# The last output tile of a fused attention and feed-forward kernel, computed by column blocks

## The chip, the cores and the metric

The kernel runs on one core of a Trainium2 chip. The metric is device microseconds of one execution; the figure given for a kernel is the median over runs. Engines are TensorE (PE in the profile; its weight loads are PEld), VectorE (DVE), ScalarE (ACT), GpSimd (POOL) and SyncE (SP), which issues the stores.

## What is computed

Attention in a sliding window over 8 batches of 8 heads, 576 positions and 64 dimensions, whose output, as 4608 rows of 512, goes through a two-layer network with a smooth ReLU between the layers:

```python
def _attn_ref(q, k, v):
    scores = scale * np.matmul(q, k.transpose(0, 1, 3, 2))
    mask = np.abs(pos[:, None] - pos[None, :]) <= 32
    attn = softmax(np.where(mask, scores, -1e9))
    return np.matmul(attn, v)

def _moe_ref(x, w_in, w_out):          # x: 4608 x 512, w_in: 512 x 2048, w_out: 2048 x 512
    h = x @ w_in
    g = np.where(h >= 1, h, np.where(h <= -1, 0.0, (h + 1) ** 2 / 4))
    return g @ w_out                   # 4608 x 512, float32
```

## The kernel before

The work is a software pipeline over 152 steps (the loop over `a` at the end of the kernel; 18 token blocks of 256 tokens, 8 steps each, and 8 steps more). In step `a` the first layer's product for block `t = a // 8` and 256 hidden columns `f = a % 8` is formed: eight matmuls of 256 columns into the PSUM tile `hp` (L441). ScalarE (L445) and VectorE (L447, L448) turn it into two of the 16 slices of `gT[t]`, bf16, hidden units on the partitions. Attention of later batches (scores, sums, transposes) is laid into the early and middle steps by a list written by hand (`ev`, `tps`, `xps`); its last events fall at step 128.

The second layer's product runs eight steps behind, in `quarter(x)`. The output has 36 tiles of 128 tokens by 512 columns; tile `tt` takes four calls, `x = 4 * tt` to `4 * tt + 3`. Call `ff` multiplies slices `4 * ff` to `4 * ff + 3` of `gT[tt // 2]` (the weights that are loaded, 128x128) with the rows of `w_out` (512 columns that stream), and adds to the PSUM tile `op`: four matmuls of 512 columns on L412. `op` is 128 x 512 f32, which is one PSUM bank, and the pool `ps_o` has two of them. When all 16 slices are summed, ScalarE copies the tile to SBUF (`osb`, L417, three buffers) and SyncE stores it (L418), 256 KB in 128 rows of 2 KB. SyncE's queue holds nothing else near the end.

In steps 144 to 151 there is no first-layer work any more: the eight calls for tiles 34 and 35 run one after the other. Tile 35 is the last, calls 140 to 143 in steps 148 to 151. After it stand the closing waits and the barrier of the program (L494), where SyncE waits for each DMA semaphore in turn.

All engines take their instructions in program order; the order is the order of the calls, and the waits between engines follow from the tiles that the instructions write and read.

Of the kernel before, what the change touches and what calls it, by code (L numbers as in the profile page):

```python
# [15 lines left out]
def kernel(  # L16
# [19 lines left out]
    nc = tc.nc  # L36
    B, H, S, D = q.shape
    NT, DM, DFF = out.shape[0], 512, 2048
# [31 lines left out]
    w_out = const.tile([128, 16, DM], BF, name="w_out")  # L70
# [4 lines left out]
    V, P, A = nc.vector, nc.gpsimd, nc.scalar  # L75
# [287 lines left out]
    NF = DFF // 256  # L363
# [39 lines left out]
    gT, op = {}, {}  # L403

    def quarter(x):

        tt, ff = divmod(x, 4)
        if tt not in op:
            op[tt] = ps_o.tile([128, DM], FP, name="op", tag="op"), []
        o, done = op[tt]  # L410
        for j in range(4 * ff, 4 * ff + 4):
            nc.tensor.matmul(o, gT[tt // 2][:, j, 128 * (tt % 2):128 * (tt % 2) + 128], w_out[:, j],  # L412
                             start=not done, stop=len(done) == 2 * NF - 1, skip_group_check=True)
            done.append(j)
        if len(done) == 2 * NF:
            osb = osp.tile([128, DM], FP, name="osb")
            A.copy(osb, o)  # L417
            nc.sync.dma_start(out=out[128 * tt:128 * tt + 128, :], in_=osb)  # L418

    for a in range(NF * NB + NF):  # L420
        t, f = divmod(a, NF)
# [27 lines left out]
        for x in pre:  # L449
            quarter(x)  # L450
# [9 lines left out]
        for x in post:  # L460
            quarter(x)
# [37 lines left out]
```

## Time and profile before

| what | us |
|---|---|
| median of 4 runs | 323.26 |
| lowest, highest | 322.52, 324.16 |
| the profiled execution | 323.3 |
| its span (first to last instruction) | 321.5 |
| TensorE busy | 306.4 (95%) |
| VectorE busy | 246.5 (77%) |
| ScalarE busy | 194.5 (60%) |
| 576 matmuls of L412, busy | 146.6 |
| one copy of an output tile (L417) | 0.58 |
| one store of an output tile, issue to landing, median | 2.4 |

The profile is of one execution. [...] The chain of waits follows the work that ended last back from the end. A line in a timeline gives start, length, engine, line, what is written and read, how many, and in brackets how long the engine stood idle before and who ended that.

### The profile page before, as it was taken

To read this page: it belongs to the slowest core of one execution; us is meant where nothing else is said; L and a number is where in the kernel's file an instruction comes from. 1 tells how busy PE (TensorE), PEld (TensorE's weight loads), DVE (VectorE), ACT (ScalarE), POOL (GpSimd) and SP (SyncE) were. 2 spreads that over 40 slices of the span, in tenths; PEclk is the share of its full clock that TensorE was granted. 3 is DMA by queue.
4 is the path that set the end of the run, shared out by engine and by line. 5 is a ranking of instruction groups with operands and counts; after the bars stand their busy time and mean duration, and the time that the engine had idled before them with its cause. 6 is when DMAs were issued, how large, how long until landed. Compare 5 with 4: busy or idle time off the path is not lost.

```text
span 321.5 us, 8537 instructions
## 1 busy us (share of the span) xinstructions
PE 306.4 (95%) x3643; PEld 202.2 (63%) x3643; DVE 246.5 (77%) x384; ACT 194.5 (60%) x320; POOL 86.3 (27%) x120
## 2 busy tenths in 40 slices
PE   8949799999999999999999999999999999999995
PEld 3537655666666666666666666666666666666652
DVE  2335975887888898888888888888888888887760
ACT  3647765676776566766666667566666766554421
POOL 8972937897204603222320300000000000000000
PEclk9998999999999999999999999999999999999999
DMA  9999999999999999929991936005320010000111
GB/s 147 141 155 190 146 176 124 200 151 165 151 162 157 165 125 178 160 55 101 191 162 47 108 87 128 35 33 108 79 65 33 35 35 36 33 35 33 46 54 65
DMA packets 121029, 34.52 MB, mean 107 GB/s; under 512 B 108704, under 2 KB 116128, under 8 KB 120992
## 3 DMA queue, kind: packets, MB, share of 16 engines
q0 software_dynamic: 92128, 18.06, 72.5%
q1 hardware_dynamic: 28864, 15.93, 20.5%
q8 instruction: 28, 0.46, 0.6%
q14 instruction: 9, 0.07, 0.1%
HBM read 36.70 MB, written 9.44 MB: 143 GB/s over the span
## 4 chain that ended last, share of the span: by engine, by line
PE 83%; DVE 5%; DMA 3%; ACT 3%; POOL 3%; issue 1%; POOLq 0%; ACTq 0%
PE op L412 38%; PE hp L441 36%; PE bb L284 6%; DMA w_in<-in_moe_w_in_dram 3%; PE bb L218 2%; DVE mx L447 2%; DVE gT L448 1%; POOL vn L101 1%; PE tp L179 1%; POOL kn L85 1%; DVE xT L296 1%; ACT lr L290 1%; ACT rc L291 1%; ACT pt L226 1%; POOL w_in L105 1%
## 5 line engine op out<-in xcount | busy, mean ns | idle before, releaser
L441 PE MATMUL hp<-xT,w_in 128*128 128x256 bf16 x1152 | 150.2, 274 | 4.1 <-DVE xT L299 1.3
L412 PE MATMUL op<-w_out,gT 128*128 128x512 bf16 x576 | 146.6, 380 | 0.0
L445 ACT ACTIVATE rr<-hp 128x512 f32<-128x512 f32 x144 | 85.5, 595 | 91.8 <-PE hp L441 88.5
L441 PEld LDWEIGHTS <-w_in 128*128 128x128 bf16 x1152 | 111.9, 98 | 46.2 <-issue 4.8
L447 DVE TENSOR_TENSOR mx<-hp,rr 128x512 f32<-128x512 f32 x144 | 99.3, 690 | 42.5 <-ACT rr L445 40.3
L448 DVE SCALAR_TENSOR_TENSOR gT<-rr,mx 128x512 bf16<-128x512 f32 x144 | 99.7, 692 | 4.9
L412 PEld LDWEIGHTS <-gT 128*128 128x128 bf16 x576 | 53.2, 98 | 41.7
L226 ACT ACTIVATE pt<-bb 128x1024 bf16<-128x1024 f32 (+1 forms) x33 | 33.1, 1010 | 6.0 <-PE bb L218 4.8
L101 POOL DMA_DIRECT2D vn<-in_v_dram x32 | 27.6, 882 | 30.3 <-PE bb L218 28.9
L296 DVE TENSOR_TENSOR xT<-bb,rc 128x512 bf16<-128x512 f32 (+1 forms) x32 | 21.1, 658 | 11.3 <-ACT rc L291 10.8
L417 ACT COPY osb<-op 128x512 f32<-128x512 f32 x36 | 20.8, 581 | 11.6 <-PE op L412 11.2
L291 ACT ACTIVATE rc<-lr 128x512 f32<-128x512 f32 (+2 forms) x40 | 23.5, 587 | 1.3
L93 POOL DMA_DIRECT2D qn<-in_q_dram x10 | 12.3, 1240 | 40.8 <-DMA qT<-qn 40.8
L290 ACT ACTIVATE lr<-bb 128x512 f32<-128x512 f32 (+2 forms) x40 | 22.0, 550 | 1.4 <-PE bb L284 1.3
L193 DVE TENSOR_TENSOR pt<-pt,mask 128x1024 bf16<-128x1024 bf16 (+1 forms) x34 | 20.9, 616 | 0.2 <-ACT pt L226 0.2
L284 PE MATMUL bb<-pt,ones 64*64 64x256 bf16 (+3 forms) x352 | 19.5, 256 | 1.5 <-DVE xT L296 0.6
L284 PE MATMUL bb<-pt,vn 64*64 64x128 bf16 (+3 forms) x712 | 18.2, 204 | 0.0
L284 PEld LDWEIGHTS <-ones 64*64 64x64 bf16 x352 | 10.5, 105 | 10.4 <-issue 9.4
L284 PEld LDWEIGHTS <-vn 64*64 64x64 bf16 x712 | 16.7, 107 | 0.0
L85 POOL DMA_DIRECT2D kn<-in_k_dram x24 | 13.0, 554 | 11.0 <-DMA w_in<-in_moe_w_in_dram 3.2
L218 PE MATMUL bb<-qT,kT 64*64 64x128 bf16 x520 | 13.4, 220 | 0.8 <-DVE kT L182 0.8
L93 POOL DMA_DIRECT2D kn<-in_k_dram x10 | 12.1, 1219 | 3.3 <-DMA kn<-in_k_dram 1.9
(44 smaller groups left out, 98.1 us busy)
## 6 DMA issues: line engine op xcount, KB each, us to landing
out_dram<-osb SPq DMA_DIRECT2D x36, 256.0 KB, 2.4
vn<-in_v_dram POOLq DMA_DIRECT2D x32, 144.0 KB, 5.1
qn<-in_q_dram POOLq DMA_DIRECT2D x10, 288.0 KB, 7.5
kn<-in_k_dram POOLq DMA_DIRECT2D x10, 288.0 KB, 8.9
w_out<-in_moe_w_out_dram POOLq DMA_DIRECT2D x4, 512.0 KB, 9.5
kn<-in_k_dram POOLq DMA_DIRECT2D x24, 72.0 KB, 4.8
w_in<-in_moe_w_in_dram POOLq DMA_DIRECT2D x6, 256.0 KB, 7.6
qn<-in_q_dram POOLq DMA_DIRECT2D x20, 72.0 KB, 4.7
```

The costliest lines, as they stand in the source:

```text
L93: nc.gpsimd.dma_start(out=x[:, :, h], in_=src[b, NY * h:NY * h + NY].rearrange("y s d -> (y s) d") .rearrange("(u p) d -> p u d", p=128))
L101: nc.gpsimd.dma_start(out=vn[b][64 * a:64 * a + 64, :, h], in_=v[b, y:y + 2].rearrange("y s d -> (y s) d") .rearrange("(c r) d -> r c d", ...
L226: A.activation(p, ps[:, :, :128 * n].rearrange(like, y=m), AF.Exp, scale=D ** -0.5)
L284: nc.tensor.matmul(bb[HD[h], a, o + c0:o + c1], ones[HD[a]] if c is None else vn[b][HD[a], c, h], p(a, h), start=n == 0, stop=True, skip_g ...
L290: A.activation(lr[:, :, :D0], bb[:, :, D0:2 * D0], AF.Ln)
L291: A.activation(rc[:, :, :D0], lr[:, :, :D0], AF.Exp, scale=-1.0)
L296: muls.append(lambda: V.tensor_mul(o, bb[:, :, :D0], rc[:, :, :D0]))
L412: nc.tensor.matmul(o, gT[tt // 2][:, j, 128 * (tt % 2):128 * (tt % 2) + 128], w_out[:, j], start=not done, stop=len(done) == 2 * NF - 1, s ...
L441: nc.tensor.matmul(hp[:, j], w_in[:, kk, 256 * f + 128 * j:256 * f + 128 * j + 128], xT[:, kk, r0:r0 + TB], start=n == 0, stop=n == 3)
L445: A.activation(rr, hp, AF.Relu, scale=0.5, bias=0.5)
L447: V.tensor_max(mx, hp, rr)
L448: V.scalar_tensor_tensor(gT[t][:, 2 * f:2 * f + 2], rr, 1.0, mx, op0=ALU.min, op1=ALU.mult)
```

## The change

Only the last tile (`tt == 35`) is affected. Each of its four calls now does all 16 slices for 128 of the 512 output columns (block `ff`: columns `128 * ff` to `128 * ff + 127`), as 16 matmuls of 128 columns, in place of 4 slices for all 512 columns. After each call ScalarE copies these 128 columns to a new `osb` buffer and SyncE stores them, 64 KB in 128 rows of 512 bytes. All four blocks are parts of the same PSUM tile `op`. The other 35 tiles are as before.

```diff
-        for j in range(4 * ff, 4 * ff + 4):
-            nc.tensor.matmul(o, gT[tt // 2][:, j, 128 * (tt % 2):128 * (tt % 2) + 128], w_out[:, j],
-                             start=not done, stop=len(done) == 2 * NF - 1, skip_group_check=True)
+        rows, last = slice(128 * tt, 128 * tt + 128), tt == NT // 128 - 1
+        c = slice(128 * ff, 128 * ff + 128) if last else slice(0, DM)
+        for j in range(2 * NF) if last else range(4 * ff, 4 * ff + 4):
+            nc.tensor.matmul(o[:, c], gT[tt // 2][:, j, 128 * (tt % 2):128 * (tt % 2) + 128], w_out[:, j, c],
+                             start=j == 0 if last else not done, stop=j == 2 * NF - 1 if last else len(done) == 2 * NF - 1,
+                             skip_group_check=True)
             done.append(j)
-        if len(done) == 2 * NF:
+        if last or len(done) == 2 * NF:
             osb = osp.tile([128, DM], FP, name="osb")
-            A.copy(osb, o)
-            nc.sync.dma_start(out=out[128 * tt:128 * tt + 128, :], in_=osb)
+            A.copy(osb[:, c], o[:, c])
+            nc.sync.dma_start(out=out[rows, c], in_=osb[:, c])
```

In instructions: 16 matmuls of 512 columns become 64 of 128, each with its weight load; one copy of 512 columns becomes four of 128; one store becomes four.

## The prediction

> **What bounds the kernel now.** I read the page's chain of waits by line first (TensorE holds 83% of the span), then the same chain over the last 16 us, because the edit touches one output tile of 36, the last.
>
> ```profile
> 308.95 0.87 PE hp L441 x8
> 309.82 7.78 PE op L412 x36
> 317.61 0.02 issue
> 317.63 0.58 ACT osb L417
> ```
>
> The columns are start, length, what. From 309.82 on nothing is on the chain but the output product: four matmuls of an earlier quarter, then 32 of tiles 34 and 35. After these stands one copy, and then nothing that computes. So every nanosecond that the last tile gains or loses is a nanosecond of the span; there is no other work to hide it. The timeline after the last matmul starts shows the rest of the path:
>
> ```profile
> 317.21 0.38 PE L412 MATMUL op<-w_out,gT 128*128 128x512 bf16 x1
> 317.63 0.58 ACT L417 COPY osb<-op 128x512 f32<-128x512 f32 x1 [2.87 <-PE op L412]
> 318.24 0.33 SPq L418 DMA_DIRECT2D out_dram<-osb  x1
> ```
>
> The last matmul ends at 317.59, ScalarE starts 0.04 later, its copy takes 0.585, the store is issued 0.03 after it and lands 2.00 after its issue (the answer on the tile osb has 2.0). SyncE waits for it until 320.26, goes through the rest of its list of closing waits until 320.69, and the closing barrier ends at 321.5. The profiled execution took 323.3 us, 1.8 beyond its span, and stands 0.04 above the median of the four runs (323.26, from 322.52 to 324.16).
>
> The first matmul of tile 35 starts 15 pitches before the last one. The pitch follows from the 36 matmuls that run from 309.66 to 317.59: (7.93 - 0.38) / 35 = 0.216 us. So tile 35 now takes, from its first matmul to the end of its copy, 15 x 0.216 + 0.379 + 0.037 + 0.585 = 4.24 us.
>
> **The matmuls.** 16 of 512 columns become 64 of 128, so the 128x128 blocks of gT are loaded 64 times and not 16. What does a load with a matmul of 128 columns cost in a stream? One row has just this shape:
>
> ```profile
> 6.58 0.67 PE L181 MATMUL tp<-ident,qb 128*128 128x128 bf16 x9
> L181 PEld LDWEIGHTS <-qb x9: 96/98/98, 6.4 to 7.0; 128*128 128x128 bf16 x9
> L181 PE MATMUL tp<-ident,qb x9: 219/219/220, 6.6 to 7.0; 128*128 128x128 bf16 x9
> ```
>
> Nine of them take 0.67 us, and the last alone 0.22: (0.67 - 0.22) / 8 = 0.056 each, with a full load in front of every one. A load is shown as 98 ns, but loads and matmuls overlap: the pitch is a quarter of 0.216 and 2 ns more. Those nine are transposes; the upper bound for matmuls into f32 sums is a load that doesn't overlap the next, 0.098. I take 0.056. Then 63 x 0.056 + 0.220 = 3.75 stands against 15 x 0.216 + 0.379 = 3.62.
>
> [...]
>
> **The copy.** ScalarE reads 128 columns at a time. The narrowest rows of f32 from PSUM:
>
> ```profile
> L290 ACT ACTIVATE lr<-bb 128x512 f32<-128x512 f32 x16 | 9.5, 593 | 0.0
> L290 ACT ACTIVATE lr<-bb 128x384 f32<-128x384 f32 x8 | 3.9, 485 | 0.6 <-PE bb L284 0.6
> L249 ACT ACTIVATE pt<-s 128x192 bf16<-128x192 f32 x2 | 0.5, 332 | 0.0
> ```
>
> (593 - 485) / 128 = 0.84 ns for a column, so 384 columns fewer save 0.32 and a copy of 128 takes 0.585 - 0.324 = 0.26. Bounds: 0.146 (a quarter, no fixed part) and 0.332 (the row of 192). Without any wait added, tile 35 would take 3.75 + 0.037 + 0.26 = 4.05: **0.19 less than now**.
>
> **The wait that the change adds.** All four column blocks lie in one PSUM tile, one bank. Block 1 starts to be written when block 0 has to be read. In the old kernel nowhere is a PSUM tile read while TensorE still has to write into it: each reader takes a finished tile, and the next one goes to another buffer. So the trace can't show the case. The nearest row is TensorE refilling a bank that another engine is reading:
>
> ```profile
> 37.37 0.68 DVE L447 TENSOR_TENSOR mx<-hp,rr 128x512 f32<-128x512 f32 x1
> 38.11 0.27 PE L441 MATMUL hp<-xT,w_in 128*128 128x256 bf16 x1 [0.72 <-DVE mx L447]
> ```
>
> The matmul stood 0.72 us until the reader was done, and began 0.05 after its end. There the columns were the same; here they differ. Ends for the change: no wait, or the first matmul of each of blocks 1 to 3 waits for the copy of the block before. I take the wait, because the bank is the unit in that row. Queued behind the waiting matmul are the 15 others of its block, and behind these the next copy and store: all on the path. Each hand-over then costs the end of the last matmul (0.220), ScalarE's start (0.037), the copy (0.26) and TensorE's restart (0.053), less the pitch that would have been there (0.056): 0.51. **Three of them: +1.54.** With the -0.19 this makes +1.35 to the end of the last copy. The cover by the next block's matmuls that column blocks might have is thus gone; only the stores of blocks 0 to 2 lie beside later work.
>
> [...]
>
> TensorE's idle share also bears on its clock. It would stand still for about a quarter of tile 35 (1.5 of 5.6 us). In the stretch 16 to 20 us it was busy 1.88 of 4 us and the granted clock stayed 1.00, so I cost this at nothing; a halved clock over the last two blocks would add 32 x 0.056 = 1.8.
>
> **The store.** The last one carries 128 rows of 512 bytes and not of 2 KB. In the stretch 319 to 320 the old one shows:
>
> ```profile
> DMA packets 144, 0.26 MB, mean 262 GB/s; under 512 B 16, under 2 KB 16, under 8 KB 144
> q1 hardware_dynamic: 144, 0.26, 70.0%
> ```
>
> That is 0.70 us of 16 DMA engines, 8 data packets on each, 0.087 a packet. The page's row of that queue over the whole span (28864 packets, 15.93 MB, 20.5% of 16 x 321.5 us) has, after 4608 such packets are taken off, 24256 smaller ones of 268 bytes and 27 ns in the mean. On a line between the two, 512 bytes take 35 ns: 8 x 0.035 = 0.28, so the landing comes **0.42 earlier**. Bounds: nothing (a packet costs the same), -0.52 (a quarter of the time). Three more issues of 0.33 on SyncE's queue lie 1.4 us apart and wait for nobody. Each block takes a new osb of three: block 2 needs that of tile 34, whose store was issued at 314.79 and landed at 316.80, a microsecond ahead; block 3 needs that of block 0, also landed by then. No wait there.
>
> **The closing waits.** The stores take eight semaphores in turn, and SyncE's closing list asks for them in that order, 0.061 each in the trace. Now the last store has the second of the eight, and six more are asked for after it landed. Three more stores make it the fifth, with three behind it: **-0.18** (bounds 0 and -0.18).
>
> **Sum:** +1.35 - 0.42 - 0.18 = +0.75. On the profiled execution 323.3 + 0.75 = 324.05, a span of 322.25; on the median 324.0.
>
> **The rivals.**
> 1. No wait by bank. For it: the columns are disjoint. Against it: the refill row. Then -0.19 - 0.42 - 0.18 = -0.79: 322.5.
> 2. The weight loads become the bound. Place: inside each block. Price: with 0.098 a pair, 60 pitches x 0.042 = +2.5, in all +3.3: 326.5, slower. It decides from a pitch of about 0.070 on, where 60 x 0.014 lifts the sum over half a per cent. For it: the load's 98 ns; against it: the nine at 0.056.
> 3. The split does less than it says at the end: the small store lands no earlier and the list of waits is as long. Then +1.35: 324.6.
>
> **How the numbers follow.** A measurement of this kernel tells about 0.5%, 1.6 us, from no change; the four runs shown differ by that much. Chances: my forecast 0.68, at 323.3 to 324.6 by the bounds on copy and store; rival 3 0.14; rival 1 0.08; rival 2, from 0.070 on, 0.10. The range 322.8 to 325.2 holds the first two with the scatter of the runs and leaves out nearly all of the other two. Slower by over 0.5%: rival 2 and a corner where copy and store are both at their upper bounds, 0.11. Faster by over 0.5%: no case reaches it, 0.02. Within: 0.87.
>
> **What would show it.** In the new profile: three idle times of about 0.5 us before L412 matmuls, put down to the copy; a period of 1.41 us from block to block; a pitch of 0.056 inside; copies of 0.26; a last copy ending at about 319.56; its store landing about 1.6 after its issue. I am wrong if those idle times are missing, if the pitch is near 0.1, or if a copy starts before its block is done.

## The result, and the profile after

The changed kernel takes 324.42 us (median of 44 runs) beside 323.51 (63 runs of the old kernel): the ratio is 1.0032, 95% interval 1.0021 to 1.0042. That is 0.7 to 1.4 us more, where +0.75 was forecast; the measured time lies within the range, and within half a per cent of the old one.

The profiled executions differ by only 0.2 us (323.52 beside 323.3; spans 321.7 and 321.5), because the new one was 0.63 us ahead at its 48th matmul of the first layer, at about 30 us, and 0.62 at the last one. The edit doesn't touch that part of the program; in the traces below, which begin with the same code but for the last three, that 48th matmul starts anywhere from 29.65 to 31.63. So every trace below is measured from the start of the last matmul of the first layer, which the edits don't touch: 12.82 us to the end of the span now, 11.99 before. The first stage of the table takes 4.43 in every trace of this document.

| stage, us | old | changed | difference |
|---|---|---|---|
| last first-layer matmul to first matmul of tile 35 | 4.43 | 4.43 | 0.00 |
| from there to the end of the last copy | 4.24 | 5.71 | +1.47 |
| from there to the landing of the last store | 2.03 | 1.59 | -0.44 |
| from there to the end of the span | 1.30 | 1.10 | -0.20 |
| sum | 11.99 | 12.82 | **+0.83** |

The chain of the changed kernel over its last microseconds (start, length, what):

```profile
309.20 5.22 PE op L414 x36
314.42 0.02 issue
314.44 0.27 ACT osb L420
314.72 0.04 issue
314.76 1.07 PE op L414 x16
315.83 0.03 ACTq L420
315.86 0.04 issue
315.90 0.27 ACT osb L420
316.17 0.04 issue
316.21 1.07 PE op L414 x16
...
318.80 0.27 ACT osb L420
```

Where the old chain had one unbroken TensorE piece up to the single copy, matmuls and copies now alternate: 16 matmuls, a copy, 16 matmuls, with a period of 1.45 us. The waits of the same stretch say who holds whom (in total, times, longest), and below them stands TensorE's timeline:

```profile
ACT osb L420 <- PE op L414: 6.7, 5, 2.9
...
PE op L414 <- ACT osb L420: 1.1, 3, 0.4
```

```profile
314.76 1.05 PE L414 MATMUL op<-w_out,gT 128*128 128x128 bf16 x16 [0.35 <-ACT osb L420]
316.21 1.05 PE L414 MATMUL op<-w_out,gT 128*128 128x128 bf16 x16 [0.40 <-ACT osb L420]
317.66 1.05 PE L414 MATMUL op<-w_out,gT 128*128 128x128 bf16 x16 [0.40 <-ACT osb L420]
```

The wait of PE for ACT is new. TensorE, which waited for nothing in the old kernel's end, stands idle three times (0.35, 0.40, 0.40). The 16 matmuls of a block take 1.05: 15 pitches of 0.056 and 0.22 for the last one. The idle time is less than the cost of a hand-over (0.55), because the profile counts the end of the last matmul as busy (0.22 shown for it, beside a pitch of 0.056).

The last store, in the timeline and in the DMA engines between 319.9 and 320.3:

```profile
318.80 0.27 ACT L420 COPY osb<-op 128x128 f32<-128x128 f32 x1 [1.19 <-PE op L414]
319.09 0.33 SPq L421 DMA_DIRECT2D out_dram<-osb  x1
DMA packets 144, 0.07 MB, mean 164 GB/s; under 512 B 16, under 2 KB 144, under 8 KB 144
q1 hardware_dynamic: 144, 0.07, 56.4%
```

56.4% of 0.4 us is 0.23 us of each DMA engine for eight packets of 512 bytes, 28 ns each, where the old store had 0.70. It lands 1.56 after its issue (old: 2.00).

### The profile page after: what moved, and what is told of

Read it like the earlier page. It is cut to its first block, busy times and chain, and to the rows that moved or that the text cites. A ratio compares the mean times of both kernels' runs of the same rounds, so it can differ in the third digit from the quotient of the medians.

```text
span 321.7 us, 8645 instructions
## 1 busy us (share of the span) xinstructions
PE 306.6 (95%) x3691; PEld 204.2 (63%) x3691; DVE 246.6 (77%) x384; ACT 194.9 (61%) x323; POOL 86.3 (27%) x120
## 4 chain that ended last, share of the span: by engine, by line
PE 83%; DVE 5%; ACT 3%; DMA 3%; POOL 3%; issue 2%; ACTq 0%; POOLq 0%
PE op L414 38%; PE hp L444 36%; PE bb L284 6%; DMA w_in<-in_moe_w_in_dram 3%; PE bb L218 2%; DVE mx L450 2%; DVE gT L451 1%; POOL kn L85 1%; PE tp L179 1%; POOL vn L101 1%; DVE xT L296 1%; ACT lr L290 1%; ACT rc L291 1%; ACT pt L226 1%; ACT rr L448 1%
## 5 line engine op out<-in xcount | busy, mean ns | idle before, releaser
L414 PE MATMUL op<-w_out,gT 128*128 128x512 bf16 (+1 forms) x624 | 147.2, 363 | 1.1 <-ACT osb L420 1.1
L414 PEld LDWEIGHTS <-gT 128*128 128x128 bf16 x624 | 55.4, 98 | 41.6 <-issue 1.5
L420 ACT COPY osb<-op 128x512 f32<-128x512 f32 (+1 forms) x39 | 21.3, 549 | 12.6 <-PE op L414 12.2
```

The source lines that it names most:

```text
L414: nc.tensor.matmul(o[:, c], gT[tt // 2][:, j, 128 * (tt % 2):128 * (tt % 2) + 128], w_out[:, j, c], start=j == 0 if last else not done, st ...
```

## The experiments

Times to the end are from the last matmul of the first layer, as in the table. Twelve kernels were run.

### A PSUM tile for each block

```diff
+        if tt == NT // 128 - 1 and ff:
+            pool, tag = (None, (ps_h, "hp"), (ps_h, "hp"), (ps_o, "op"))[ff]
+            op[tt] = pool.tile([128, DM], FP, name="op", tag=tag), []
```

> The changed kernel, but each of the four column blocks of the last tile is summed in a PSUM tile of its own, in four different banks. Same matmuls, copies and stores. Measured from the first matmul of the last tile to the end of the span (7.56 us in the old kernel, 8.40 in the changed one). Theory A, TensorE waits because the block before is still being read in the same bank: no idle time between the blocks, last copy ends after 63 x 0.056 + 0.220 + 0.037 + 0.265 = 4.05, then 1.59 to the landing and 1.10 to the end: 6.74, so 0.8 below the old kernel (322.7 beside 323.5) and 1.7 below the changed one. Rival B, the time went into the four times as many weight loads or the four copies on ScalarE, whatever the bank: about 8.4 as in the changed kernel.

Measured: 12.04 to the end, ratio 1.0031 (1.0007 to 1.0055). Neither theory gave this. TensorE's idle time is gone: the last matmul ends 8.16 after the last first-layer one (old kernel 8.04). But ScalarE now waits, in the first fence by the timelines of both engines and the waits, in the second by the landings of the last five stores (least, median, most) and the queues between 313 and 319 (a line that joins matmuls names the shape of the first; these 68 are 4 of tile 34 and all 64 of tile 35):

```profile
312.70 4.60 PE L417 MATMUL op<-w_out,gT 128*128 128x512 bf16 x68
...
315.59 0.27 ACT L423 COPY osb<-op 128x128 f32<-128x128 f32 x1 [0.67 <-PE op L417]
317.74 0.44 ACT L423 COPY osb<-op 128x128 f32<-128x128 f32 x2 [1.88 <-DMA out_dram<-osb]
...
ACT osb L423 <- DMA out_dram<-osb: 1.9, 1, 1.9
```

```profile
DMA to landing us min/median/max: 1.6/2.1/3.3
q8 instruction: 1, 0.02, 1.1%
```

The copy of block 2 needs the SBUF buffer of tile 34. That store landed 3.27 us after its issue, not 2.0, and 1.24 after the matmuls of block 2 were done. The late landing comes with one packet of queue q8, 16 KB of instructions, which held one DMA engine from 315.21 for 1.06 us; eight 2 KB packets of the store, one engine's share, moved only from 316.27 to 317.16, after it. The old kernel has 28 such packets and none after 299.4; all kernels with four blocks or more, whose TensorE has 96 or more instructions more, have a 29th in the last tile (unused TensorE instructions bring it too: last experiment).

The runs put this kernel 0.2 to 1.8 us above the old one, the one profiled execution 0.05. Whether the landing is later still in other executions, no trace shows.

### One PSUM tile over two banks

```diff
+        last = tt == NT // 128 - 1
         if tt not in op:
-            op[tt] = ps_o.tile([128, DM], FP, name="op", tag="op"), []
+            op[tt] = two_banks(ps_s) if last else ps_o.tile([128, DM], FP, name="op", tag="op"), []
         o, done = op[tt]
+        if last:
+            o = o[:, ff % 2]
```

> The changed kernel, but the last tile is summed in one PSUM tile that spans two banks: blocks 0 and 2 in the first, 1 and 3 in the second. Theory A1, the bank is the unit of the wait: no idle time before any block (block 2 waits for the copy of block 0, which ended during block 1), first matmul to end of span 6.74 as with four tiles. Rival A2, the tile is the unit: three idle times of about 0.4 us as in the changed kernel, 8.4.

Measured: 12.83, the changed kernel's time (ratio 1.0024, 0.9997 to 1.0051). TensorE's timeline:

```profile
314.41 1.05 PE L417 MATMUL bb<-w_out,gT 128*128 128x128 bf16 x16 [0.35 <-ACT osb L423]
315.86 1.05 PE L417 MATMUL bb<-w_out,gT 128*128 128x128 bf16 x16 [0.40 <-ACT osb L423]
```

Blocks 1 and 2 wait although the copy they wait for reads another bank. So the wait is set by the tile, not by the bank: the rival holds, and the forecast's reason for the wait was wrong where its wait was right.

### The narrow copies and stores alone

The old kernel, with the finished last tile copied and stored by columns:

```diff
-            A.copy(osb, o)
-            nc.sync.dma_start(out=out[128 * tt:128 * tt + 128, :], in_=osb)
+            w = 128 if tt == NT // 128 - 1 else DM
+            for c in range(0, DM, w):
+                A.copy(osb[:, c:c + w], o[:, c:c + w])
+                nc.sync.dma_start(out=out[128 * tt:128 * tt + 128, c:c + w], in_=osb[:, c:c + w])
```

> The old kernel's matmuls (four quarters of the sum over all 512 columns), but the finished last tile is copied and stored by 128 columns at a time: the narrow copies and stores alone, with nothing for TensorE to wait for. Four copies of 0.265 take at least 1.06 where one took 0.585, and the last store is small. Theory A: the copies run faster than SyncE can issue stores (two loads at the start of the old kernel were issued 0.45 apart), so the last store goes out 3 x 0.46 after the first one and the end comes at 3.65 + 0.27 + 0.03 + 1.38 + 1.56 + 1.10 = 7.99 after the first matmul, 0.4 above the old kernel. Rival, the issues keep up with the copies: 7.5, the same as the old kernel within 0.1.

Measured: 12.46 (8.03 from the first matmul of tile 35; 7.99 expected), ratio 1.0021 (0.9998 to 1.0045). The copies take 0.77 together, less than 4 x 0.265 = 1.06, so they overlap:

```profile
316.47 0.77 ACT L419 COPY osb<-op 128x128 f32<-128x128 f32 x4 [2.87 <-PE op L412]
```

The stores go out at 316.76, 317.18, 317.66 and 318.13: the last waits 0.86 for its turn on SyncE. Narrow copies without matmuls between them lose 0.47.

### Three stores more, earlier

The old kernel, with tile 20 stored in four pieces:

```diff
+            w = 128 if tt == 20 else DM
+            for c in range(0, DM, w):
+                nc.sync.dma_start(out=out[128 * tt:128 * tt + 128, c:c + w], in_=osb[:, c:c + w])
```

> The old kernel, but tile 20, in the middle of the run, is stored in four pieces of 128 columns, so three stores more come before the last one, off the path. Theory: the last store then has the fifth of eight semaphores and three closing waits fewer follow its landing; first matmul of the last tile to end of span 7.56 - 0.19 = 7.37, everything up to the landing unchanged. Rival, the length of the closing list has nothing to do with which store is last: 7.56. The median should fall by 0.2 us, which three rounds can't separate from no change; the trace can.

Measured: 11.80, and 0.20 less after the landing (1.30 to 1.10), all before it unchanged. The times can't tell (1.0005, 0.9983 to 1.0026). SyncE's waits of the closing list, from the landing on, in the old kernel and in this one:

```profile
L494 SPq EVENT_SEMAPHORE  x7: 28/28/28, 320.3 to 320.6; - x7
```

```profile
L496 SPq EVENT_SEMAPHORE  x4: 28/28/28, 320.4 to 320.6; - x4
```

Seven became four, the one for the last store among them. This is the whole of the changed kernel's -0.20 in that stage.

### SBUF buffers of their own

To the kernel with four PSUM tiles:

```diff
-            osb = osp.tile([128, DM], FP, name="osb")
+            if last:
+                osb = osp.tile([128, DM], FP, name="osl", tag="osl", bufs=4)
+            else:
+                osb = osp.tile([128, DM], FP, name="osb")
```

> As the experiment with a PSUM tile for each block, but each of the four blocks also has an SBUF buffer of its own, so that no copy can wait for the landing of an earlier store. From the last matmul of the first layer to the end of the span the old kernel has 11.99, the changed one 12.82, four PSUM tiles with the three shared buffers 12.04. Theory A, what ate the gain there was the wait of the third copy for the store of tile 34, held up on one DMA engine by the fetch of 16 KB of instructions: the copies now start with the end of each block and the end comes at 4.43 + 3.75 + 0.04 + 0.27 + 0.03 + 1.56 + 1.10 = 11.2, 0.8 below the old kernel. Rival B, the third copy was late for another reason (ScalarE, or the fetch itself): again about 12.0.

Measured: 11.44; 322.78 us, ratio 0.9982 (0.9963 to 1.0002). The copies begin with the end of their blocks, the last ends at 8.47: theory A, by the trace; the interval of the times just holds 1. Of the 0.24 missing to 11.2, 0.22 is SyncE's: the last store went out 0.25 after its copy in place of 0.03. One issue of five took far longer (least, median, most):

```profile
L427 SPq DMA_DIRECT2D out_dram<-osl x4: 332/384/1438, 314.7 to 317.6; - x4
```

It is the store of block 1, issued at 315.57 while the instruction fetch held one DMA engine (314.95, for 1.70 us): the issue ended only at 317.01, after the fetch (316.65), and the two after it came late. That the two earlier stores, stuck behind that engine, held it up is read from these times; no run tests it alone.

### Eight blocks in one tile

The changed kernel with 64 columns a block:

```diff
-        c = slice(128 * ff, 128 * ff + 128) if last else slice(0, DM)
+        for cc in (2 * ff, 2 * ff + 1) if last else (0,):
+            c = slice(64 * cc, 64 * cc + 64) if last else slice(0, DM)
```

> The changed kernel with eight column blocks of 64 in the one PSUM tile: seven hand-overs and 128 loads. It sizes the two disputed costs. Hand-over, theory: end of the last matmul 0.2, ScalarE's start 0.08, a copy of 0.21, restart 0.05, so seven idle times of about 0.35 to 0.4, no smaller than with 128 columns although the copy is. Pitch inside a block: if the loads bind below 128 columns, it stays near 0.055 and the end comes 18.5 us after the last matmul of the first layer; if the columns still set it, 0.029 and 15.2 us.

Measured in one execution: 17.22. Between the two figures, but for other reasons. TensorE's blocks, early and late:

```profile
316.31 0.63 PE L415 MATMUL op<-w_out,gT 128*128 128x64 bf16 x16 [0.34 <-ACT osb L421]
...
319.62 0.63 PE L415 MATMUL op<-w_out,gT 128*128 128x64 bf16 x16 [1.18 <-ACT osb L421]
...
323.04 1.01 PE L415 MATMUL op<-w_out,gT 128*128 128x64 bf16 x16 [0.34 <-ACT osb L421]
```

Early blocks: (0.63 - 0.19) / 15 = 0.029 a matmul, 64 columns at nearly the rate of 512 (0.46 ns a column beside 0.216 / 512 = 0.42). So the weight loads, shown as 98 ns each here too, don't bind at 128 columns (0.056), nor at 64. Five idle times are 0.32 to 0.34, just under the 0.35 expected; two are 0.89 and 1.18, where the copy waited for a late store and its buffer. And the last two blocks run at 0.051. The granted clock says why, by stretches (PE busy, PEld, DVE, ACT, POOL, clock, DMA share, GB/s):

```profile
317.55:320.95 3.40, 1.61 (x45) 1.42 (x45) 0.00 (x0) 0.64 (x3) 0.00 (x0) 1.00 0.10 21
320.70:324.00 3.30, 2.61 (x48) 2.28 (x46) 0.00 (x0) 0.42 (x2) 0.00 (x0) 0.54 0.13 28
```

The clock was about halved from 320.95 on (0.54 over the second stretch), after a stretch with much idle time: in the 3.40 us just before, TensorE was busy 1.61 (47%), and no idle piece was over 1.18. What share or length of idle time brings this on is not shown: in the old kernel's 16 to 20 us, which the forecast used, TensorE was busy 47% too, at full clock. The rise over the changed kernel, 4.4 us, is hand-overs, these two waits, the halved clock and 0.26 more of closing waits together.

### One PSUM tile, own SBUF buffers

The changed kernel with the edit of the SBUF buffers alone.

> The changed kernel with its one PSUM tile, but the four blocks of the last tile have SBUF buffers of their own. In the changed kernel ScalarE began the copies of blocks 1 to 3 0.081 after the end of the matmuls, of block 0 0.037. Theory: the 0.044 more is the second wait instruction that the shared buffers bring; with buffers of their own all four copies begin after 0.037, the three idle times before the matmuls fall from 0.40 to 0.35, and the end comes 12.82 - 3 x 0.044 = 12.69 after the last matmul of the first layer. Rival: the delay comes with the shared PSUM tile, 12.82.

Measured in one execution: 12.70, theory. TensorE's three idle times:

```profile
314.59 1.05 PE L414 MATMUL op<-w_out,gT 128*128 128x128 bf16 x16 [0.35 <-ACT osl L423]
316.00 1.05 PE L414 MATMUL op<-w_out,gT 128*128 128x128 bf16 x16 [0.35 <-ACT osl L423]
317.41 1.05 PE L414 MATMUL op<-w_out,gT 128*128 128x128 bf16 x16 [0.35 <-ACT osl L423]
```

All four copies begin 0.037 after their matmuls. With this, the period is 1.407, against 1.41 in the forecast.

### Two blocks, 384 and 128

The kernel with PSUM and SBUF tiles of their own, and

```diff
-        c = slice(128 * ff, 128 * ff + 128) if last else slice(0, DM)
+        if last and ff in (1, 3):
+            return
+        c = slice(0, 384) if last and ff == 0 else slice(384, DM) if last else slice(0, DM)
```

> Two column blocks in the last tile, 384 and then 128 columns, each in a PSUM tile and an SBUF buffer of its own: 32 matmuls, two copies, two stores. Theory: no idle time of TensorE, pitches 0.162 and 0.056, the last copy of 128 columns and the small last store as with four blocks; one store more than the old kernel leaves five closing waits behind the landing. End after the last matmul of the first layer: 4.43 + 3.65 + 0.04 + 0.27 + 0.03 + 1.56 + 1.23 = 11.2, 0.8 below the old kernel (322.6 beside 323.4). Rival: the small last store or the copy behind the large one is late, 12 or more.

Measured: 11.24, **322.53 us beside 323.43, ratio 0.9976 (0.9957 to 0.9994)**: faster than the old kernel by 0.1 to 0.4%, and so than the changed one, which was slower than the old. TensorE, ScalarE and SyncE:

```profile
312.83 5.60 PE L419 MATMUL op<-w_out,gT 128*128 128x512 bf16 x41
317.58 0.48 ACT L428 COPY osl<-op 128x384 f32<-128x384 f32 x1 [2.01 <-PE op L419]
318.47 0.27 ACT L428 COPY osl<-op 128x128 f32<-128x128 f32 x1 [0.41 <-PE op L419]
318.08 1.01 SPq L429 DMA_DIRECT2D out_dram<-osl  x2
```

The large copy ends 0.4 before the small one begins, TensorE never waits, and with 64 instructions fewer than four blocks need there is no 29th fetch.

### The last of the eight semaphores

The same, with the stores of tiles 20 to 24 cut in two:

```diff
-            nc.sync.dma_start(out=out[rows, c], in_=osb[:, c])
+            for cs in (slice(0, 256), slice(256, DM)) if 20 <= tt < 25 else (c,):
+                nc.sync.dma_start(out=out[rows, cs], in_=osb[:, cs])
```

> The two blocks of 384 and 128 columns with buffers of their own, and the stores of tiles 20 to 24 cut in two, so that five stores more come before the last one and it has the last of the eight semaphores: nothing but the closing barrier follows its landing. End after the last matmul of the first layer: 11.2 less 5 x 0.062 = 10.9, 1.1 below the old kernel, 0.3%. Rival: the extra stores in the middle delay the middle of the run by what the end gains.

Measured: 10.91 to the end, 0.92 of it after the landing. The time is 322.60, ratio 0.9978 (0.9960 to 0.9997): faster than the old kernel, but not to be told from the kernel without the cuts. Whether the cuts cost something in the middle stays open at this size.

### The instruction fetch put back

To the kernel with 384 and 128 columns, 40, 13 and 11 unused matmuls at the start of the program, to move the fetch:

```diff
+        z = ps_h.tile([128, 512], FP, name="z", tag="hp")
+        for _ in range(40):
+            nc.tensor.matmul(z[:, :16], warm[:, :128], warm[:, :16], start=True, stop=True)
```

> The kernel with blocks of 384 and 128 columns and buffers of their own, and 40 matmuls of 16 columns more at the start of the program (an unused product, into a free PSUM tile), so that TensorE has 80 instructions more. Theory: each 256 instructions of TensorE cost a fetch of 16 KB through one DMA engine; the 80 more bring a fetch back into the last 10 us, which the kernel without them has not, and the store that is under way then lands late, at 3 to 4 us after its issue in place of 2.0. Rival: the late stores of the kernels with four blocks had to do with the small rows or with four stores in a row; then no fetch appears and the store of tile 34 lands after 2.0.

Measured with 40, in one execution: a fetch came at 309.50, before the store of tile 34 was issued; that store landed after 2.01, so this run doesn't tell the two apart. The 256 instructions of the theory hold in the old kernel's trace as a mean only: from its first fetch (11.34) to its 28th (299.36) TensorE did 3437 matmuls and 3436 loads, 255 for each of 27 fetches, with 92 to 374 between single ones. In the changed kernel it is 253 for each of 28.

> The kernel with blocks of 384 and 128 columns, and 13 unused matmuls of 16 columns at the start of the program. With 40 of them a fetch came back, but at 0.1 us after the last matmul of the first layer, between two stores. 54 instructions of TensorE fewer put it 27 matmuls later, at about 5.6, when the store of tile 34 (issued at 5.2) moves its packets. Theory: one DMA engine is held up for 1.0 to 1.7 us and that store lands 3 to 4 us after its issue in place of 2.0. Rival, late stores came from the small rows or from four stores in a row: it lands after 2.0 although the fetch is there.

> The same with 11 unused matmuls: the fetch two matmuls later, at about 5.9, still ahead of the packets of the store of tile 34 (6.1 to 6.8). Theory: that store lands 3 to 4 us after its issue; rival: 2.0. If no fetch appears at all, the end of the program was reached first and this kernel says nothing.

Measured with 13 and 11, one execution each: fetches at 314.25 and 315.39 (5.13 and 5.43 after the last matmul of the first layer), 1.03 and 1.04 long; the store of tile 34 landed after 2.37 and 2.68. These lines show the second one's store and its queue:

```profile
DMA to landing us min/median/max: 2.7/2.7/2.7
q8 instruction: 1, 0.02, 1.1%
```

There are no four small stores here, and the landing is late with the fetch and at 2.0 without: the fetch delays a store that is under way. By 0.4 and 0.7 us, though, not by 1 to 2 as expected. The traces say why: what counts is when the fetch ends. In every kernel where it fell on the store of tile 34, the landing came 1.4 to 1.5 us after its end (us after the last matmul of the first layer):

| kernel | fetch ends | store of tile 34 lands | between | issue to landing |
|---|---|---|---|---|
| 13 unused matmuls | 6.16 | 7.60 | 1.44 | 2.37 |
| 11 unused matmuls | 6.46 | 7.92 | 1.45 | 2.68 |
| four PSUM tiles | 7.14 | 8.51 | 1.37 | 3.27 |
| four PSUM tiles, own buffers | 7.78 | 9.24 | 1.47 | 4.01 |

So the four small stores aren't needed for a landing of 3 to 4 us. The old kernel has no such stores and shows it too: its store issued at 297.44 landed 4.33 later, 1.48 after the end of the fetch at 300.29 (one view of the store, one of its queue from 298 to 302):

```profile
DMA to landing us min/median/max: 4.3/4.3/4.3
q8 instruction: 1, 0.02, 1.5%
```

The ends (11.26, 11.25) are as without the fetch, since here nothing waits for that buffer.

## Why the prediction was right

By its steps:

- **The last tile's end is the kernel's end.** Right: +0.83 in the trace, all of it behind the first matmul of tile 35; +0.75 was forecast. The runs (0.7 to 1.4) hold both. By parts: +1.47, -0.44 and -0.20, where +1.35, -0.42 and -0.18 were forecast.
- **Pitch 0.056 with full weight loads.** Right: 15 pitches take 0.84 in each block, and even at 64 columns the columns set it (0.029). The nine transposes' row, 0.056, holds for these matmuls too.
- **Copy of 128 columns 0.26.** Right, 0.265.
- **The wait.** Right in number, and in size but for ScalarE's start (below); wrong in its reason. I wrote "because the bank is the unit in that row"; with two banks in one tile the waits were the same, so the tile is the unit. The row could not show that, as tile and bank were one there. That the forecast came out although its reason was wrong is luck in this one point: in the edit, too, tile and bank were one.
- **ScalarE's start 0.037 before each copy.** Wrong for blocks 1 to 3: 0.081. Before these copies a wait instruction for the shared SBUF buffer ends only after the matmuls (ACTq in the chain above); block 0's was over 0.87 before its copy. With buffers of their own there is none, and the delay is gone. 3 x 0.044 = 0.13 of the sum.
- **The clock, costed at nothing.** Right: from 314.4 to 320 TensorE was busy 3.17 of 5.60 us, and the granted clock stayed 1.00. That the idle share bears on the clock was my reading of the old kernel's trace: the clock was 0.50 from 24 to 26 us, where TensorE was busy throughout, after 0.69 busy of the 5.17 us up to 23.17, and 0.51 from 320 to 321, where it stood idle. How much idle time it takes is not shown.
- **The store.** Right: -0.44 beside -0.42. The packet was cheaper than on my line (28 ns, not 35).
- **The closing waits.** Right: -0.20 beside -0.18, and shown alone.
- **"No wait there" for the SBUF buffers.** Right in the changed kernel, but with less cover than I wrote: the store of block 0 landed after 3.51, and block 3 needed its buffer only 0.5 after that. The forecast had no term for the instruction fetch that fell on that store (315.80, 1.37 long); that it cost nothing here was luck.

Rival 1 (no wait, -0.79) did not come true in the changed kernel, and its price is not had by taking the wait away alone. In the traces PSUM tiles of their own give +0.05, with SBUF buffers too -0.55, with two uneven blocks -0.75. What it left out is what the wait had hidden: at the faster pace the next thing late is a buffer that a store has not left, and then SyncE's queue. Rival 2 falls with the pitch, rival 3 with the last store (-0.44) and the closing waits (-0.20).

## What to carry to other kernels

Give each column block of the last tile its own accumulator tile and its own output buffer: parts of one tile are handed over in turn, and each hand-over costs the end of a matmul, a copy and two starts, here half a microsecond (0.55). Even so, four blocks gained 0.55 us in the trace and the times don't tell them from no change; a large first block and a small last one gained 0.75 us in the trace and 0.1 to 0.4% in the times, with the short copy and store and fewer instructions. Count what comes after the last landing too: closing waits on semaphores that follow the last store's are on the path (three of them cost 0.20 us here).

## What the runs showed of the hardware

- The fetch of 16 KB of instructions takes one DMA engine 0.9 to 1.8 us in the last 25 us of these traces and delays the packets of a store on that engine: of a store of 256 KB one engine's eight packets follow it, and the store lands 1.4 to 1.5 us after its end (2.4 to 4.3 us after the issue in place of 2.0). One store issue beside it took 1.44 in place of 0.33. In the kernels with four PSUM tiles TensorE had no idle time beside it (68 matmuls in one piece of 4.60 us, 67 in one of 4.38), but stores were late (3.27 and 4.01 us).
- In the kernel with eight blocks TensorE's clock fell to about half (0.54 from 320.70 to 324.00) after 3.40 us with 1.61 busy and no idle piece over 1.18; in the changed kernel, busy 1.05 of every 1.45 us, it stayed full (1.00). Where the border lies is open.
- Stores in a row leave SyncE 0.42 to 0.48 apart (316.76, 317.18, 317.66 and 318.13 with the narrow copies alone).
